# Three visits of the attention made whole, and a fourth half product that accumulates in an old bank

## Chip, cores and metric

The kernel runs on one core of one Trainium2 chip. The metric is device microseconds of that core; three runs of the kernel before gave 557.68, 557.76 and 559.34 us, the median is 557.76.

## What is computed

A causal attention with decay, in 4 batches, 8 heads, 768 tokens of 64, is followed by a feed-forward layer on the 3072 rows of 512 that it gives:

```
state = lam**64 * state + (k * decay).T @ v        # per head, block after block of 64 tokens
out   = tril(q @ k.T * decay) @ v + (q * decay) @ state
h     = max(out_rows @ w_in, 0)                    # 3072 x 512 @ 512 x 2048
y     = (h * h) @ w_out                            # 3072 x 2048 @ 2048 x 512
```

Products of the feed-forward layer are made of two halves of each operand (high and low part), three products each, to keep fp32 precision.

## The kernel before, in words

The tokens are cut into 24 chunks of 128. Eight chunks go through the feed-forward layer plainly, in three tiles (`ffn`, matmuls at L763 to L772). The other 16 form two **twins** of eight chunks. For a twin, four pairs of chunks stand side by side as 512 columns, and each of the two big products is done as a two-by-two block product with seven half products in place of eight. The sums of token rows that this needs are written by `pairs` into `pa`, `pz`, `ps`, `pt` (L847, L848, L855); the sums of weights are made by `differences` (L822 to L834), stored in HBM (`kept`, L812), and streamed back in pieces of 256 KB, one for each half product, into six buffers `b` (`streamed`, L870). SP issues these loads in the order of the products, and each waits for the product that last used its buffer.

`first_products` makes the hidden blocks of one pair j of weight blocks from the products 1 to 7. One **product** is six matmuls of 128x512 at L489. Products 1, 6 and 7 accumulate one after the other in the same PSUM bank, x, and ScalarE copies the bank's state away after each (`copy`, L891: r1, r2, r3). Product 2 has bank y, product 5 bank v; product 3 goes on top of 5 in v. A hidden block is the sum of a bank and a copy, made by VectorE (`block`, L895), and then ReLU and square on ScalarE (L896, L897). Product 4 has a bank of its own, z, and its block is z plus r3. `second_products` does the same for the second layer (splits at L942 and L943, sums at L950, ends at L1024).

The rest of the attention is done in between, in **visits**. A visit finishes two old chunks and opens two new ones: first half of the old results, opening of the first new chunk, second half of the old results, opening of the second new chunk, all of them small 64x64 matmuls at L489. Between the halves of the old results two tiny ScalarE copies out of the banks (L709, `dots`) order the second half behind the first. An opening is followed by VectorE work on its banks (L566, L575), a ScalarE copy of one bank (L559), and the finished results are scaled by L599. The loads of the next visit's chunks (L515, four of 512 KB: `ka` and `qv` of each chunk) wait for the buffers that this visit frees; `qv` is weighted by L539 when it lands.

Visits 1 to 8 are **parted**: the first half of the old results and the first opening are one stretch, the rest a second stretch, with four other pieces of TensorE's work between. Visits 6, 7 and 8 lie among the first twin's first products, before the products with the numbers in `INSIDE`, and their second stretch comes `LATER_BY` = 4 products later.

The order of instructions is static: `Plan.order` simulates the engines with costs written in the kernel and emits the program in the order that it finds. TensorE's order in the twins is fixed by `link`/`linked`; the order on the other engines follows from the plan's times and keys.

Of the kernel before, what the change touches and what calls it, by code (L numbers as in the profile page):

```python
# [13 lines left out]
AF = mybir.ActivationFunctionType  # L14
# [10 lines left out]
NF = DFF // P  # L25
# [11 lines left out]
WIDE, NARROW = 4 * C, 3 * C  # L37
# [192 lines left out]


VISITS = [(1, 8, 0), (1, 12, 1), (1, 14, 0)]
PARTED = {1: 1, 2: 1, 3: 1, 4: 1, 5: 1, 6: 1, 7: 1, 8: 1}
BETWEEN = {3: 3, 4: 7, 5: 11}
APART, LATER_BY = 3, 4
PAIR_LATER = [717, 726, 735, 753]
PAIR_AT = [7, 10, 13, 12]
INSIDE = {6: 9, 7: 31, 8: 52, 9: 63}

FIRST_ORDER = [1, 2, 6, 5, 7, 4, 3]  # L240
PARTS = 9
# [1 line left out]
N_RS = 2  # L243
DIFF_AT = [[440, 450, 530, 560, 565.5, 569.5, 573.5, 577.5], [590, 626, 630, 638, 646, 654, 662, 670]]
SPARE_FROM, SPARE_KEY = 16, 0.0
AT_ONCE = [1, 2, 4, 6, 5, 7, 3]
LAST_ORDER = [4, 1, 2, 6, 5, 7, 3]
KEPT = {1: 0, 2: 1, 5: 2, 4: 3, 7: 4, 6: 5, 3: 6}
A_PROD, PASS = 1.36, 10.9
# [23 lines left out]
def tt(n):  # L273

    return 0.066 + n / 960


def act(n):

    return 0.085 + n / 1200  # L280
# [13 lines left out]
def kernel(ctx: ExitStack, tc: tile.TileContext, ka, qv, lamx, w, out):  # L294
    nc = tc.nc
    ps = ctx.enter_context(tc.tile_pool(name="ps", bufs=1, space=PSUM))
    plan = Plan()
# [5 lines left out]
    def place(name, at, shape, dtype=F32):  # L303

        n = 1
        for m in shape:
            n *= m
        a = nc.alloc_sbuf_tensor_at(name, [P, n], dtype, offset=BASE + 4 * at).ap()
        if len(shape) == 2:
            a = a.rearrange("p (a b) -> p a b", a=shape[0])  # L310
        if len(shape) == 3:
            a = a.rearrange("p (a b c) -> p a b c", a=shape[0], b=shape[1])
        return a
# [61 lines left out]
    sums = {g: place(f"p{g}", REGIONS[f"p{g}"][0], [2, n, WIDE], F32R) for g, n in (("a", 4), ("z", 2), ("s", 4), ("t", 4))}  # L375
# [11 lines left out]
    def at(b):  # L387
        return tiles[b.kind][b.slot]
# [99 lines left out]
    def mm(*args, **kw):  # L488
        nc.tensor.matmul(*args, **kw, skip_group_check=True)  # L489
# [376 lines left out]
    def streamed(i, j, k, key):  # L866

        n_streams[i] += 1
        b = Buf("b2" if i == 0 and B2_FROM <= n_streams[0] <= 7 * B2_STEPS and n_streams[0] % 4 == 0 else "b")
        return b, in_turn("streamed", plan.op("SP", LOAD, key - 12, lambda: nc.sync.dma_start(out=at(b).bitcast(F32), in_=kept[i][j][KEPT[k]]), stored[i, j], [b], lat=3.2))  # L870

    def first_products(p, j, key):

        banks, r, h, made = {k: Buf("bank") for k in "xyvz"}, [Buf("u") for _ in range(3)], hidden[p], ready_h[p]
        where = {1: "x", 2: "y", 6: "x", 5: "v", 7: "x", 4: "z", 3: "v"}
        source = {1: ("a", 0), 2: ("a", 2), 4: ("z", 0), 6: ("s", 0), 3: ("s", 2), 7: ("t", 0), 5: ("t", 2)}
        st = {}

        def product(i, deps=()):
            (b, o), bank, (g, k) = streamed(0, j, i, key), banks[where[i]], source[i]  # L880

            def fn():
                x, first = sums[g][:, :, k:k + 2], i in (1, 2, 5, 4)
                for t, (u, v) in enumerate(((0, 0), (0, 1), (1, 0))):
                    for kb in range(2):
                        mm(at(bank), at(b)[:, u, kb * P:kb * P + P], x[:, v, kb], start=first and not t and not kb, stop=t == 2 and kb == 1)

            return link(plan.op("PE", A_PROD, key, fn, [o] + ready2[p][g] + list(deps), [b, bank, p_[p][g]], mode="F", entries=12))

        def copy(k, dst, o):  # L890
            return plan.op("ACT", act(WIDE) + 0.09, key - 6, lambda: nc.scalar.copy(at(dst), at(banks[k])), [o], [banks[k], dst])  # L891

        def block(k, t, f, a, deps):
            b = h[t, f]
            o = plan.op("DVE", tt(WIDE) + 0.1, key - 6, lambda: nc.vector.tensor_tensor(out=at(b), in0=at(banks[k]), in1=at(a), op=ALU.add), deps, [banks[k], b, a])  # L895
            o1 = plan.op("ACT", act(WIDE) + 0.12, key, lambda: nc.scalar.activation(at(b), at(b), AF.Relu), [o], [b])  # L896
            o1 = plan.op("ACT", act(WIDE) + 0.12, key, lambda: nc.scalar.activation(at(b), at(b), AF.Square), [o1], [b])  # L897
            made[t, f] = [o1]
            return o

        def run(i):
            f0, f1 = 2 * j, 2 * j + 1
            if i == 1:
                st["r1"] = copy("x", r[0], product(1))
            if i == 2:
                block("y", 0, f0, r[0], [product(2), st["r1"]])
            if i == 6:
                st["r2"] = copy("x", r[1], product(6, [st["r1"]]))
            if i == 5:
                st["p5"] = product(5)  # L910
            if i == 7:
                st["r3"] = copy("x", r[2], product(7, [st["r2"]]))
                st["v"] = block("v", 1, f1, r[2], [st["p5"], st["r3"]])
            if i == 4:
                st["p4"] = product(4)
            if "r3" in st and "p4" in st:
                block("z", 1, f0, r[2], [st.pop("p4"), st["r3"]])
            if i == 3:
                block("v", 0, f1, r[1], [product(3, [st["v"]]), st["r2"]])

        return run
# [119 lines left out]
    for f in range(NF):  # L1041
        t = FIRST + f * SLOW_STEP
# [5 lines left out]
    def place_of(v):  # L1048
        if v < len(VISITS):
            k, f, _ = VISITS[v]  # L1050
            return begin[k] + per[k] * f
        if v in BETWEEN:
            return begin[2] + per[2] * BETWEEN[v]
        return twice[0][0] + INSIDE[v] * A_PROD

    chunks = []
    for i in range(len(CHUNKS)):
        ti = PLACE[i][0]
        if i < N_ALONE:
            key = 0 if ti == 0 else BEGIN2  # L1060
        else:
            key = place_of((i - N_ALONE) // 2)
# [10 lines left out]
    def visiting(v, narrow, key, ahead=0):  # L1073
        old = later[max(0, 2 * v - 2):2 * v]
        chain = visit(old, later[2 * v:2 * v + 2], key, ahead, PARTED.get(v), narrow)
        for ch in old:
# [19 lines left out]
    for v, ((ti, f, ahead), chain) in enumerate(zip(VISITS, visits)):  # L1096
        chain[0].after += [steps[ti, f - ahead][2], steps[ti, f + 1][0]]
        steps[ti, f][1].after.append(steps[ti, f + 1][0])
        k = PARTED.get(v, -1)
        steps[ti, f + 1 - ahead][1].after.append(chain[k])  # L1100
        later_ = [steps[ti, f + 2][0]] if f + 2 < NF else [steps[ti + 1, g][0] for g in range(2)]
        if v in PARTED:
            chain[k + 1].after.append(steps[ti, f + 1 - ahead][1] if len(later_) == 1 else later_[0])
# [10 lines left out]
    def link(o):  # L1114
        o.after.append(end[0])
        end[0] = o
        return o

    def linked(chain):
        chain[0].after.append(end[0])  # L1120
        end[0] = chain[-1]
# [7 lines left out]
    while left:  # L1129
        g, k = left.pop(0)  # L1130
        link(steps[2, g][k])
        if k == 2 and g in visit_of:
            v = visit_of[g]
            chain = visiting(v, False, begin[2] + per[2] * g)
            n = PARTED.get(v)
            if n is None:
# [7 lines left out]
    hidden = [{(t, f): Buf(f"h{t}{f}") for t in range(2) for f in range(NF)} for _ in range(TWINS)]  # L1144
    ready_h, gate = [{} for _ in range(TWINS)], [[] for _ in range(TWINS)]
    visit_at = {k: v for v, k in INSIDE.items()}
    for p in range(TWINS):
        a, b = twice[p]
        runs = [first_products(p, j, a + 7 * A_PROD * j) for j in range(NF // 2)]
        order = [(j, i) for j in range(NF // 2) for i in (FIRST_ORDER if j or p else AT_ONCE)]  # L1150
        for j in range(1, NF // 2):
            k = order.index((j, 1))
            order[k - 1], order[k] = order[k], order[k - 1]
        n, rest = 0, []

        def visited():
            if rest and n == rest[0][0]:
                linked(rest.pop(0)[1])
            if p == 0 and n in visit_at:
                v = visit_at[n]  # L1160
                chain = visiting(v, False, a + A_PROD * n)
                k = PARTED.get(v, len(chain) - 1) + 1
                linked(chain[:k])
                if k < len(chain):
                    rest.append((n + LATER_BY, chain[k:]))

        product, after = second_products(p, b)
        for j, i in order:
            visited()
            if (j, i) == order[-1]:  # L1170
                product(LAST_ORDER[0], 0, b)
            runs[j](i)
            if j == NF // 2 - 1 and i in (2, 6, 3):
                gate[p].append(end[0])
            n += 1
            if p == 0 and n == 1:
                for k in tail:
                    link(steps[2, k[0]][k[1]])
        for k, i in enumerate(LAST_ORDER):
            for j in range(NF // 2):  # L1180
                visited()
                if k or j:
                    product(i, j, b + PASS * k + A_PROD * j)
                n += 1
            after(i)
# [63 lines left out]
```

## Time and profile before

| what | value |
|---|---|
| median of three runs | 557.76 us (557.68 to 559.34) |
| span of the profiled execution | 556.8 us |
| median less that span | 0.96 us |
| TensorE (PE) busy | 550.3 us |
| VectorE (DVE) busy | 440.8 us |
| ScalarE (ACT) busy | 339.1 us |
| mean granted TensorE clock | 0.999 |
| first twin's first products, with visits 6 to 8 | about 230 to 324 us of the span |

The profile page gives the span of the one execution that was profiled and no other time of it; the difference to the median is what lies around the span. The page's busy share of TensorE counts matmuls that overlap, so it tells only whether the engine stood empty. To see lost time, one takes the starts of matmuls: within a product they are 0.227 us apart, and a product starts 1.36 us after the one before it, unless something lies between.

### The profile page before, as it was taken

Reading aid. Unit: us, or ns where it says so; the run is one execution under the profiler, and the core shown is the slowest. Engines: PE = TensorE matmul, PEld = TensorE weight load, DVE = VectorE, ACT = ScalarE, POOL = GpSimd, SP = SyncE. Lnnn points to the kernel's source line nnn. Section 1 sums busy time; section 2 is a strip of 40 time slices with the busy share of each in tenths; the row PEclk is TensorE's granted clock in tenths of the full one; section 3 lists DMA queues with packets and bytes.
Section 4 is the critical chain, followed back from the end, with each engine's and each line's share of the span. In section 5 each row is a group of like instructions: output and inputs, shape, how many; then the busy total and the mean of one; then the engine's idle time right before and its main releaser. Section 6 shows DMA issues by size and latency. Waiting matters only on the chain.

```text
span 556.8 us, 12879 instructions
## 1 busy us (share of the span) xinstructions
PE 550.3 (99%) x4907; PEld 468.8 (84%) x4907; DVE 440.8 (79%) x867; ACT 339.1 (61%) x695; POOL 5.1 (1%) x10
## 2 busy tenths in 40 slices
PE   8999999999999999999999999999999999999997
PEld 7789899998989888888887888888888888888885
DVE  5998999997989899889686899998723235889664
ACT  5866677673644556576766856564366667754551
POOL 3000000000000000000000000000000000000000
PEclk9999999999999999999999999999999999999999
DMA  8999789875968577699989655776876666666765
GB/s 316 368 295 354 253 262 298 293 230 159 333 229 301 186 263 279 214 298 360 306 288 361 213 161 156 211 218 197 277 223 193 193 195 196 192 191 201 223 197 172
DMA packets 70141, 137.17 MB, mean 246 GB/s; under 512 B 7232, under 2 KB 19776, under 8 KB 70080
## 3 DMA queue, kind: packets, MB, share of 16 engines
q1 hardware_dynamic: 69792, 136.21, 75.6%
q8 instruction: 39, 0.64, 0.5%
q10 hardware_dynamic: 288, 0.14, 0.1%
q14 instruction: 22, 0.18, 0.1%
HBM read 100.67 MB, written 35.65 MB: 245 GB/s over the span
## 4 chain that ended last, share of the span: by engine, by line
PE 96%; DMA 2%; DVE 1%; SPq 0%; issue 0%; ACT 0%; DVEq 0%
PE bank L489 63%; PE bank L763 16%; PE bank L769 5%; PE bank L772 5%; PE bank L770 5%; DMA b<-kept 1%; DMA ka<-ka 1%; PE bank L747 1%; PE bank L742 1%; SPq L515 0%; DVE end L1024 0%; PE bank L408 0%; PE bank L425 0%; DVE h L895 0%; DVE pt L848 0%
## 5 line engine op out<-in xcount | busy, mean ns | idle before, releaser
L489 PE MATMUL bank<-v,b 128*128 128x512 f32 x672 | 153.4, 389 | 0.0
L489 PEld LDWEIGHTS bank<-v,b 128*128 128x128 f32 x672 | 126.0, 188 | 26.2
L942 ACT CAST v<-h 128x512 fp32r<-128x512 f32 x112 | 68.4, 621 | 56.9 <-PE bank L489 41.7
L895 DVE TENSOR_TENSOR h<-bank,u 128x512 f32<-128x512 f32 x64 | 44.1, 691 | 61.5 <-ACT u L891 33.3
L943 DVE TENSOR_TENSOR v<-h,v 128x512 fp32r<-128x512 f32 x112 | 75.9, 689 | 18.6 <-ACT v L942 9.2
L896 ACT ACTIVATE h<-h 128x512 f32<-128x512 f32 x64 | 40.2, 631 | 21.9 <-DVE h L895 19.5
L769 PE MATMUL bank<-wo,gh 128*128 128x512 f32 x125 | 49.3, 394 | 0.0
L489 PE MATMUL bank<-ps,b 128*128 128x512 f32 x192 | 49.1, 391 | 0.0
L489 PE MATMUL bank<-pa,b 128*128 128x512 f32 x192 | 48.8, 390 | 0.2 <-DMA b<-kept 0.2
L770 PE MATMUL bank<-wo,gh 128*128 128x512 f32 x125 | 49.0, 392 | 0.0
L891 ACT COPY u<-bank 128x512 f32<-128x512 f32 x48 | 28.0, 583 | 31.0 <-PE bank L489 30.8
L489 PE MATMUL bank<-pt,b 128*128 128x512 f32 x192 | 46.4, 390 | 0.0
L950 DVE TENSOR_TENSOR h<-h,h 128x512 f32<-128x512 f32 x64 | 43.0, 684 | 0.1
L489 PEld LDWEIGHTS bank<-pa,b 128*128 128x128 f32 x192 | 35.9, 188 | 8.0 <-DVE h L895 0.6
L489 PEld LDWEIGHTS bank<-ps,b 128*128 128x128 f32 x192 | 35.8, 188 | 7.9 <-DVE h L895 0.5
L489 PEld LDWEIGHTS bank<-pt,b 128*128 128x128 f32 x192 | 35.9, 188 | 7.5
L897 ACT ACTIVATE h<-h 128x512 f32<-128x512 f32 x64 | 38.5, 625 | 0.3
L763 PE MATMUL bank<-xb,wi 128*128 128x384 f32 x192 | 35.4, 336 | 0.0
L763 PEld LDWEIGHTS bank<-xb,wi 128*128 128x128 f32 x192 | 33.6, 188 | 0.9
L763 PE MATMUL bank<-xa,wi 128*128 128x384 f32 x180 | 34.0, 338 | 0.0
L763 PEld LDWEIGHTS bank<-xa,wi 128*128 128x128 f32 x180 | 31.6, 188 | 1.3 <-DVE work L463 0.2
L489 PE MATMUL bank<-qv,ka 64*64 64x64 f32 (+2 forms) x1040 | 26.8, 225 | 0.7 <-DMA ka<-ka 0.5
(152 smaller groups left out, 866.8 us busy)
## 6 DMA issues: line engine op xcount, KB each, us to landing
b<-kept SPq DMA_DIRECT2D x224, 256.0 KB, 2.9
work<-w SPq DMA_DIRECT2D x32, 512.0 KB, 4.8
ka<-ka SPq DMA_DIRECT2D x23, 512.0 KB, 5.4
qv<-qv SPq DMA_DIRECT2D x19, 512.0 KB, 5.5
kept<-part SPq DMA_DIRECT2D x36, 256.0 KB, 3.6
kept<-v SPq DMA_DIRECT2D x28, 256.0 KB, 4.4
kept<-wi SPq DMA_DIRECT2D x24, 256.0 KB, 3.9
kept<-wo SPq DMA_DIRECT2D x24, 256.0 KB, 3.7
```

The lines of the kernel that those rows point to most:

```text
L489: nc.tensor.matmul(*args, **kw, skip_group_check=True)
L763: nc.tensor.matmul(at(h)[:, 0:n], wt[:, cc, :], xt[:, cc, :], start=k == 0, stop=k == 3 * NCC - 1)
L769: nc.tensor.matmul(at(os_[j]), at(gh)[:, sl], woh[f], start=f == 0 and ti >= SINGLE, stop=False)
L770: nc.tensor.matmul(at(os_[j]), at(gh)[:, sl], wol[f], start=False, stop=False)
L772: nc.tensor.matmul(at(os_[j]), at(gl)[:, sl], woh[f], start=False, stop=f == NF - 1)
L891: return plan.op("ACT", act(WIDE) + 0.09, key - 6, lambda: nc.scalar.copy(at(dst), at(banks[k])), [o], [banks[k], dst])
L895: o = plan.op("DVE", tt(WIDE) + 0.1, key - 6, lambda: nc.vector.tensor_tensor(out=at(b), in0=at(banks[k]), in1=at(a), op=ALU.add), deps, [ ...
L896: o1 = plan.op("ACT", act(WIDE) + 0.12, key, lambda: nc.scalar.activation(at(b), at(b), AF.Relu), [o], [b])
L897: o1 = plan.op("ACT", act(WIDE) + 0.12, key, lambda: nc.scalar.activation(at(b), at(b), AF.Square), [o1], [b])
L942: oh = plan.op("ACT", act(WIDE) + 0.12, key - 16, lambda: nc.scalar.copy(rounded[hi.slot], at(b)), made[t, 2 * j + e], [b, hi], after)
L943: ol = plan.op("DVE", tt(WIDE) + 0.1, key - 16, lambda: nc.vector.tensor_tensor(out=rounded[lo.slot], in0=at(b), in1=rounded[hi.slot], op= ...
L950: made[o] = [plan.op("DVE", tt(WIDE) + 0.1, when, lambda: nc.vector.tensor_tensor(out=at(h[o]), in0=at(h[a]), in1=at(h[b]), op=op), deps + ...
```

## The change

Four edits. (1) Visits 6, 7 and 8 are no longer in `PARTED`: all four of their parts run in one stretch, before products 7, 29 and 49 in place of 9, 31 and 52 (and 4 later). (2) Product 4 loses its bank z and accumulates in bank x on top of 1, 6 and 7; it has to wait for the copy r3, and its block needs no sum on VectorE: ScalarE takes the ReLU straight from the bank. (3) The next pair's product 1 moves ahead by one more place, to between 7 and 4; the very first pair takes the usual order 1, 2, 6, 5, 7, 4, 3 in place of 1, 2, 4, 6, 5, 7, 3. (4) In the last pair the first of the second products stands ahead of 4 in place of ahead of 3, and the marks in the order (`gate`) that let the first splits start shift with it.

```diff
-PARTED = {1: 1, 2: 1, 3: 1, 4: 1, 5: 1, 6: 1, 7: 1, 8: 1}
+PARTED = {1: 1, 2: 1, 3: 1, 4: 1, 5: 1}
-INSIDE = {6: 9, 7: 31, 8: 52, 9: 63}
+INSIDE = {6: 7, 7: 29, 8: 49, 9: 63}
-AT_ONCE = [1, 2, 4, 6, 5, 7, 3]
+AT_ONCE = [1, 2, 6, 5, 7, 4, 3]
...
-        where = {1: "x", 2: "y", 6: "x", 5: "v", 7: "x", 4: "z", 3: "v"}
+        where = {1: "x", 2: "y", 6: "x", 5: "v", 7: "x", 4: "x", 3: "v"}
...
-                x, first = sums[g][:, :, k:k + 2], i in (1, 2, 5, 4)
+                x, first = sums[g][:, :, k:k + 2], i in (1, 2, 5)
...
-            o1 = plan.op("ACT", act(WIDE) + 0.12, key, lambda: nc.scalar.activation(at(b), at(b), AF.Relu), [o], [b])
-            o1 = plan.op("ACT", act(WIDE) + 0.12, key, lambda: nc.scalar.activation(at(b), at(b), AF.Square), [o1], [b])
-            made[t, f] = [o1]
+            squared(t, f, plan.op("ACT", act(WIDE) + 0.12, key, lambda: nc.scalar.activation(at(b), at(b), AF.Relu), [o], [b]))
             return o
+
+        def squared(t, f, o):
+            b = h[t, f]
+            made[t, f] = [plan.op("ACT", act(WIDE) + 0.12, key, lambda: nc.scalar.activation(at(b), at(b), AF.Square), [o], [b])]
...
             if i == 4:
-                st["p4"] = product(4)
-            if "r3" in st and "p4" in st:
-                block("z", 1, f0, r[2], [st.pop("p4"), st["r3"]])
+                b, o = h[1, f0], product(4, [st["r3"]])
+                squared(1, f0, plan.op("ACT", act(WIDE) + 0.12, key - 6, lambda: nc.scalar.activation(at(b), at(banks["x"]), AF.Relu), [o], [banks["x"], b]))
...
             k = order.index((j, 1))
-            order[k - 1], order[k] = order[k], order[k - 1]
+            order.insert(k - 2, order.pop(k))
...
-            if (j, i) == order[-1]:
+            if (j, i) == order[-2]:
                 product(LAST_ORDER[0], 0, b)
             runs[j](i)
-            if j == NF // 2 - 1 and i in (2, 6, 3):
+            if j == NF // 2 - 1 and i in (2, 7, 4):
                 gate[p].append(end[0])
```

**First place: TensorE at the start of the first twin, up to visit 6.** A row with `pa`, `pz`, `ps` or `pt` is a product (the sum of tokens that it reads, and its streamed buffer `b`); 64x64 rows belong to the visit. Before:

```order
L489 MATMUL bank_62<-pa,b_167 128x512 x6
L489 MATMUL bank_63<-pz,b_168 128x512 x6
L489 MATMUL bank_60<-ps,b_169 128x512 x6
L489 MATMUL bank_64<-pt,b_170 128x512 x6
L489 MATMUL bank_60<-pt,b_171 128x512 x6
L489 MATMUL bank_58<-pa,b_166 128x512 x6
L489 MATMUL bank_64<-ps,b_0_172 128x512 x6
L489 MATMUL bank_61<-pa,b_167 128x512 x6
L489 MATMUL bank_65<-work,qv_111 64x64 x2
```

These are products 2, 4, 6, 5, 7, the next pair's 1, then 3, the next pair's 2, and the first row of the visit. With the change:

```order
L489 MATMUL bank_62<-pa,b_167 128x512 x6
L489 MATMUL bank_60<-ps,b_168 128x512 x6
L489 MATMUL bank_63<-pt,b_169 128x512 x6
L489 MATMUL bank_60<-pt,b_170 128x512 x6
L489 MATMUL bank_64<-pa,b_171 128x512 x6
L489 MATMUL bank_60<-pz,b_166 128x512 x6
L489 MATMUL bank_58<-work,qv_111 64x64 x2
```

Now the products are 2, 6, 5, 7, the next pair's 1, and 4 in the bank of 6 and 7; then the visit starts, and product 3 comes behind the whole of it. Inside that visit the first opening (`qv_110,ka_108`) is now followed at once by the second half of the old results:

```order
L489 MATMUL bank_65<-qv_110,ka_108 64x64 x2
L489 MATMUL bank_59<-qv_110,ka_108 64x64 x2
L489 MATMUL bank_65<-qv_110,ka_108 64x64 x8
L489 MATMUL bank_58<-work,qv_111 64x64 x2
L489 MATMUL bank_61<-work 64x64 x2
```

Four products stood at this joint before.

**Second place: ScalarE around the same visit.** `small` rows are the two copies that the second half of the old results waits for. Before:

```order
L896 ACTIVATE h_0_200<-h_0_200 128x512
L897 ACTIVATE h_0_201<-h_0_201 128x512
L897 ACTIVATE h_0_200<-h_0_200 128x512
L896 ACTIVATE h_0_185<-h_0_185 128x512
L897 ACTIVATE h_0_185<-h_0_185 128x512
L709 COPY small<-bank_65 128x1
L709 COPY small<-bank_59 128x1
```

With the change:

```order
L891 COPY u_221<-bank_64 128x512
L896 ACTIVATE h_0_201<-h_0_201 128x512
L833 CAST v_230<-ob_106 128x256
L918 ACTIVATE h_0_200<-bank_60 128x512
L901 ACTIVATE h_0_201<-h_0_201 128x512
L709 COPY small<-bank_58 128x1
L709 COPY small<-bank_61 128x1
```

L918 is the ReLU of product 4's block straight from the bank, and L901 the square; the two copies stand directly behind them.

**Third place: SP's queue behind visit 7,** where the loads for visit 8 (`ka`, `qv`) stand among the streamed loads `b` and the stores of weight sums (`kept`). Before:

```order
L515 DMA ka_108<-ka 128x1024
L870 DMA b_167<-kept_159 128x512
L812 DMA kept_160<-v_230 128x512
L812 DMA kept_160<-v_231 128x512
L870 DMA b_168<-kept_159 128x512
L812 DMA kept_160<-v_229 128x512
L870 DMA b_169<-kept_159 128x512
L870 DMA b_170<-kept_159 128x512
L515 DMA qv_110<-qv 128x1024
L515 DMA ka_109<-ka 128x1024
L515 DMA qv_112<-qv 128x1024
L870 DMA b_171<-kept_159 128x512
```

With the change:

```order
L870 DMA b_170<-kept_159 128x512
L812 DMA kept_160<-v_226 128x512
L515 DMA ka_108<-ka 128x1024
L515 DMA qv_110<-qv 128x1024
L515 DMA ka_109<-ka 128x1024
L870 DMA b_171<-kept_159 128x512
L515 DMA qv_112<-qv 128x1024
L870 DMA b_166<-kept_159 128x512
```

The four loads now stand together, with one streamed load ahead of the last; before, one stood apart and three together.

## Rows read from the trace of the kernel before

**Rows 1.** The page's head and part 1: busy time of each engine.

```profile
span 556.8 us, 12879 instructions
...
PE 550.3 (99%) x4907; PEld 468.8 (84%) x4907; DVE 440.8 (79%) x867; ACT 339.1 (61%) x695; POOL 5.1 (1%) x10
```

**Rows 2.** Chain of waits, 226 to 400 us: start us, length us, what.

```profile
232.82 6.81 PE bank L489 x30
...
239.66 0.60 ACT u L891
...
240.28 0.70 DVE h L895
...
241.02 48.76 PE bank L489 x670
...
289.80 6.81 DMA b<-kept
...
296.75 103.40 PE bank L489 x789
```

**Rows 3.** Timeline of PE around visit 6's first stretch: start us, length us.

```profile
239.46 1.52 PE L489 MATMUL bank<-pa,b 128*128 128x512 f32 x6
241.02 1.66 PE L489 MATMUL bank<-ps,b 128*128 128x512 f32 x6
242.52 1.52 PE L489 MATMUL bank<-pa,b 128*128 128x512 f32 x6
243.97 0.27 PE L489 MATMUL bank<-work,qv 64*64 64x64 f32 x2
...
244.07 0.23 PE L489 MATMUL bank<-work,qv 64*64 64x64 f32 x2
...
244.13 0.23 PE L489 MATMUL bank<-work,qv 64*64 64x64 f32 x2
...
244.95 1.11 PE L489 MATMUL bank<-qv,ka 64*64 64x64 f32 x48
245.99 1.66 PE L489 MATMUL bank<-ps,b 128*128 128x512 f32 x6
247.49 2.88 PE L489 MATMUL bank<-pt,b 128*128 128x512 f32 x12
```

**Rows 4.** Timeline of PE at the end of visit 6's second stretch.

```profile
252.64 1.11 PE L489 MATMUL bank<-qv,ka 64*64 64x64 f32 x64
253.69 1.66 PE L489 MATMUL bank<-pa,b 128*128 128x512 f32 x6
```

**Rows 5.** Timeline of PE, 294 to 301 us.

```profile
295.05 1.52 PE L489 MATMUL bank<-pz,b 128*128 128x512 f32 x6
296.75 1.62 PE L489 MATMUL bank<-pa,b 128*128 128x512 f32 x6 [0.18 <-DMA b<-kept]
298.21 1.54 PE L489 MATMUL bank<-ps,b 128*128 128x512 f32 x6
299.59 1.52 PE L489 MATMUL bank<-pa,b 128*128 128x512 f32 x6
```

**Rows 6.** Groups of ACT, 230 to 320 us (busy us, mean ns | idle before), and one timeline row.

```profile
L896 ACT ACTIVATE h<-h 128x512 f32<-128x512 f32 x31 | 19.3, 630 | 9.5 <-DVE h L895 8.9
L833 ACT CAST v<-ob 128x256 fp32r<-128x256 f32 x28 | 10.5, 404 | 1.6 <-DVE ob L830 1.5
L709 ACT COPY small<-bank 128x1 f32<-128x1 f32 x6 | 0.7, 161 | 0.3 <-PE bank L489 0.3
...
241.50 1.16 ACT L896 ACTIVATE h<-h 128x512 f32<-128x512 f32 x2
```

**Rows 7.** Landing of the L515 loads, and stretches: PE busy, clock, DMA share, GB/s.

```profile
DMA to landing us min/median/max: 3.6/5.5/8.4
...
24.00:32.00 8.00, 8.00 (x161) 1.00 0.85 290
...
251.60:253.80 2.20, 2.20 (x130) 1.00 1.03 370
```

More of the change, by code (lines that the diff above doesn't have):

```diff
@@ L872, in first_products @@
     def first_products(p, j, key):
-        banks, r, h, made = {k: Buf("bank") for k in "xyvz"}, [Buf("u") for _ in range(3)], hidden[p], ready_h[p]
-        where = {1: "x", 2: "y", 6: "x", 5: "v", 7: "x", 4: "z", 3: "v"}
+        banks, r, h, made = {k: Buf("bank") for k in "xyv"}, [Buf("u") for _ in range(3)], hidden[p], ready_h[p]
+        where = {1: "x", 2: "y", 6: "x", 5: "v", 7: "x", 4: "x", 3: "v"}
         source = {1: ("a", 0), 2: ("a", 2), 4: ("z", 0), 6: ("s", 0), 3: ("s", 2), 7: ("t", 0), 5: ("t", 2)}
```

## The prediction, on record before the result was known

> **What bounds the kernel now.** I read the page first: TensorE is busy 550.3 of 556.8 us, VectorE 440.8, ScalarE 339.1 [rows 1]. So work taken from VectorE is worth nothing by itself; only what lets TensorE start its matmuls earlier counts. Busy time can't show that, as matmuls overlap, so I went on to the chain of waits in the stretch that the change touches. There the chain is TensorE alone but for two places: at 239.66 it leaves TensorE for a copy r3 on ScalarE and a block sum on VectorE, and at 289.80 for a streamed load of 6.81 us [rows 2]. Last I read TensorE's timeline and measured from start to start. A product takes 1.36 us (six times 0.227; 30 matmuls in 6.81 us [rows 2]). From 296.75 on, the first twin's 103.4 us of chain have no wait but the borders of visits [rows 2]. So the change can save only what these starts show as lost.
>
> **Borders of a stretch.** At visit 6's first stretch four things are lost [rows 3, 4]. The product ahead of it takes 242.52 to 243.97, 1.45 us, 0.09 too much. Its small matmuls come in fours, 0.06 us apart (244.07 to 244.13), but the first four take 0.10: 0.04 lost. At the end of the second stretch 64 matmuls from 252.64, sixteen fours of 0.058, would be issued by 253.58; the next product starts at 253.69: 0.11 lost. That product, as 245.99 to 247.49 shows, takes 1.50 us: 0.14 lost. Together 0.38 us for each stretch, whatever its length. Three visits become one stretch each in place of two: 3 x 0.38 = **1.14 us** saved. The small matmuls stay the same, 2.02 us a stretch (243.97 to 245.99), so a whole visit takes about 4.0.
>
> The new joint, first opening then second half of the old results, is in no row. The nearest joint is that from the half results to the opening inside a stretch: 244.95 follows in the same rhythm, at no cost [rows 3]. The other end is a border, 0.38. I take nothing, since both sides of the joint are 64x64 matmuls as in the nearest row. The Trainium skill says the same in "TensorEngine Tiling (Array Packing)", Key Properties: changing the tiling mode drains the engine, changing only the tile doesn't; by it, too, the joint is free.
>
> **First wait, 240.8 us.** Product 3 of the first pair should have started at 239.46 + 1.36 = 240.82 and started at 241.02: 0.20 lost, and it took 1.50, 0.14 more [rows 3]. It waited for the block sum in bank v, which waited for r3 (0.60, then 0.70 [rows 2]); the order gave it one product (the next pair's 1) as cover, 1.36 us, too little for 0.16 of matmul tail, 0.60, 0.70 and three handovers of some 0.03. In the new order the next pair's 1 and product 4, then all of visit 6, stand between 7 and 3: the wait goes, **0.34 us** saved.
>
> **Second wait, 296.4 us.** The product after 295.05 was due at 296.41, started at 296.75 and took 1.46, the next one 1.38 [rows 5]: 0.34 + 0.10 + 0.02 = **0.46 us** lost to a streamed load issued behind visit 8's big loads [rows 2]. A buffer b is refilled when its product ends and used again five products later, so a load has 6.8 us, less about 0.2; 6.81 is just too long. With the change three of four big loads can be issued inside visit 7, when TensorE uses no b. Walk it from the visit's start, T: `ka` at T + 2.0 (after the first opening), `qv` at T + 3, `ka` at T + 4, b_171 when the first product behind the visit ends, T + 5.6, the other `qv` behind it, b_166 at T + 7. The shortest landing of such a load is 3.6 us, and at the 370 GB/s of a full stretch 512 KB take 1.4 us and 256 KB 0.7 [rows 7]. With 0.7 for a store ahead of it `ka` lands by T + 6.3, then 7.7, 9.1, b_171 at 9.8, `qv` 11.2, b_166 11.9. Needed: b_171 at T + 4.2 + 6 x 1.36 = T + 12.4, b_166 at T + 13.7. Some 2 us are left, which cover two or three more stores. I take the wait as gone. The bounds are all of it kept, and a stall longer by one more 512 KB in the bunch, 1.4.
>
> **Product 4 in bank x.** It removes 16 sums on VectorE of 0.70 [rows 2], 11.2 us, worth nothing on the path (VectorE is not what TensorE waits for once the first wait is gone). It adds a wait of TensorE for r3, 16 times, with one product between 7 and 4. The copy starts at once in the trace (product 7's last matmul, then 239.66 [rows 2]): 0.16 of tail, 0.60 of copy, two handovers, 0.84 in all against 1.36. Each has 0.5 us to spare, so nothing; the cover is that next product 1 (the first second product in the last pair). The same distance stands between 6 and 7 in the kernel before, 16 times, and the chain shows no wait there. What is late next if the copy is late is product 4 and all of TensorE behind it.
>
> **The whole visit.** Its second half needs the two tiny copies. For visit 6: product 4 now stands at 239.46, the visit starts at 240.91, and the first opening ends at 242.93. ScalarE has, from 239.62 on, a copy (0.60), a ReLU (0.63), a cast (0.40, which waits for VectorE), the ReLU from the bank, not before 240.98, a square, and two copies of 0.16 [rows 6]. One behind the other the last ends at 242.8; as two ReLUs take 1.16 [rows 6], not 1.26, it is earlier. Margin 0.1 to 0.4 us, so nothing, but thin; the bound is one ScalarE operation late. The banks hold: six for the visit, one for v, one for the next x, and the second opening's last bank is x, free after that ReLU, 2 us ahead. All four loads must be in at the start of a visit; they have 22 products, some 30 us. The second products' first splits have three products of cover in place of four, 4.1 us against two operations of about 0.7: nothing.
>
> **Sum.** 1.14 + 0.34 + 0.46 = 1.94 us, all in the span: 556.8 to 554.9. The median stands 0.96 above the span, so 557.76 - 1.94 = **555.8 us**, 0.35% faster. About 0.3%, 1.7 us, is what a measurement of this kernel can tell from no change, so this lies on its edge.
>
> **Rivals.**
> - *The tiny copies come late.* One ScalarE operation (0.63) less the margin, some 0.4, plus 0.14 for the restart, 0.54 a visit: 1.6 given back, 557.4. For it: the square stands ahead of them in the queue, and a cast that waits for VectorE. Against: the margin. In part, 0.4 to 1.6, chance 0.19.
> - *The streamed loads still wait.* 0.46 stays: 556.3; with the longer bunch 557.2. For it: four loads together, where three were too many. Against: the walk. Chance 0.15.
> - *The joint costs a border,* 3 x 0.38: 557.0. Chance 0.04.
> - *Slower: product 4 waits for r3.* The order on ScalarE is new, and the first twin's casts [rows 6] can stand ahead of a copy. Two operations ahead of it (0.63 + 0.40) make 0.84 into 1.87, 0.51 over the cover, with 0.14 of restart 0.65 for each product 4. In all eight pairs of the first twin that is 5.2 us: 561.0. It decides against the change once the 16 average over 0.23 us, as 1.94 + 1.7 are then used up. Chance 0.08.
> - *Slower: the clock falls.* A stretch of small matmuls twice as long could let the granted clock drop to 1.2 GHz. Against: it was 1.00, the 2.4 GHz level, through 251.6 to 253.8 and through 24 to 32 us, eight microseconds of small matmuls [rows 7]. At half rate for three products behind each visit it would cost 3 x 4.1 = 12.2 us: 568.0. Chance 0.02. The rule behind it is in the Trainium skill, "TensorE: Matmul & The Clock Gate", Part 1: the half rate is the default and activity releases it; the rows here speak against a fall.
>
> That the change doesn't do what it says is out: the order shows it.
>
> **How the numbers follow.** The forecast has 0.52: all three gains, 555.3 to 556.3 with the run's own scatter, of which 0.46 lie beyond 0.3% (below 556.1). The tiny copies, the loads and the joint (0.38) end within 0.3%, as does the upper end of the forecast (0.06). The two slower cases hold 0.10. The range goes from 555.3 to 557.4, the whole price of the late copies, and leaves out about 0.12.
>
> **What would show it.** Right: in TensorE's timeline one stretch of about 4.0 us for each of visits 6 to 8, with its parts unbroken; no gap near 241 and none from a load near 290 to 300; VectorE's L895 down from 64 to 48 with no change elsewhere; second twin unchanged. Wrong: waits of TensorE for L709, for L891 ahead of `pz` products, or for `b<-kept`, or a granted clock below 1.00 behind a visit.

## The result: slower, 564.33 us

Six runs of the changed kernel took 562.38 to 566.21 us, median 564.33; six of the kernel before, 557.68 to 559.34, median 557.82. The ratio is 1.0112, with the interval 1.0098 to 1.0126: the change costs 6.5 us (564.33 less 557.82), where the forecast was a gain of 1.94. The profiled run took 564.42 us with a span of 562.3, 5.5 longer than before [rows 1]. Between a run's time and its span lie 1.7 to 2.2 us in all profiled runs of this study; the 0.96 in the prediction came from the median and another execution's span, and nothing hangs on it, as the sum was a difference. That difference is 2.1 in all six runs of the changed kernel and 1.7 to 1.8 in the runs of the kernel before, so some 0.4 of the 6.5 us lies outside the span, where no run shows a cause.

The page of the changed kernel: head, busy time, the queue that carries instructions, the chain's shares, and the group of the block sums.

```profile
span 562.3 us, 12859 instructions
...
PE 551.5 (98%) x4907; PEld 470.7 (84%) x4907; DVE 430.6 (77%) x851; ACT 338.3 (60%) x695; POOL 5.1 (1%) x10
...
q8 instruction: 39, 0.64, 0.4%
...
PE 98%; issue 1%; DVE 0%; DVEq 0%
...
L895 DVE TENSOR_TENSOR h<-bank,u 128x512 f32<-128x512 f32 x48 | 33.2, 691 | 69.4 <-ACT u L891 33.9
```

VectorE lost its 16 sums and some 10 us, as intended, and TensorE's busy time is 1.2 us up [rows 1]. In the chain "issue" has grown from 0 to 1%: time in which TensorE waited for nothing that the profile shows. TensorE's list of waits in the changed kernel (who waited for whom: us in total, times, longest us) has four of these, 5.4 us together, and one wait of the program's start:

```profile
PE bank L489 <- issue: 5.4, 4, 2.5
PE bank L408 <- DVE ob L392: 1.5, 1, 1.5
```

The chain of waits in the stretch of [rows 2] says where:

```profile
232.76 10.88 PE bank L489 x189
243.65 2.48 issue
246.13 35.66 PE bank L489 x375
281.79 1.19 issue
282.98 31.70 PE bank L489 x378
314.68 1.56 issue
316.24 103.90 PE bank L489 x643
```

The detours over ScalarE, VectorE and the streamed load [rows 2] are gone; in their place stand three **stops** of TensorE, 2.48, 1.19 and 1.56 us, 5.23 in all, one in each whole visit. TensorE's timeline in visit 6 (start us, length us) answers to [rows 3, 4]:

```profile
241.83 0.94 PE L489 MATMUL bank<-qv,ka 64*64 64x64 f32 x42
...
243.37 0.28 PE L489 MATMUL bank<-qv,work 64*64 64x64 f32 x2
246.13 0.27 PE L489 MATMUL bank<-work 64*64 64x64 f32 x2 [2.48 <-issue]
...
246.52 1.82 PE L489 MATMUL bank<-qv,ka 64*64 64x64 f32 x62
248.28 2.46 PE L489 MATMUL bank<-ps,b 128*128 128x512 f32 x6
```

And in visit 7:

```profile
280.21 1.11 PE L489 MATMUL bank<-qv,ka 64*64 64x64 f32 x64
281.15 0.65 PE L489 MATMUL bank<-s,qv 64*64 64x64 f32 x32
282.98 0.34 PE L489 MATMUL bank<-qv,hold 64*64 64x64 f32 x8 [1.19 <-issue]
```

The joint itself is free: 281.15 follows the opening in the same rhythm. The stop comes deeper, in the middle of the second half of the old results; in visit 6 matmuls on both sides of it read tiles of the same names. And behind visit 6's stop things are slow: 62 small matmuls take 1.82 us where 64 took 1.11 [rows 4], the product 2.46 where it took 1.66 [rows 3]. The stretches of the changed kernel show why (busy time of PE, PEld, DVE, ACT, POOL, then granted clock, DMA share, GB/s):

```profile
241.00:243.60 2.60, 2.60 (x156) 2.51 (x152) 1.04 (x3) 2.58 (x8) 0.00 (x0) 1.00 0.97 314
243.60:246.10 2.50, 0.05 (x1) 0.00 (x0) 0.47 (x2) 0.00 (x0) 0.00 (x0) 1.00 0.96 318
246.10:250.00 3.90, 3.87 (x88) 3.46 (x89) 2.71 (x6) 0.00 (x0) 0.00 (x0) 0.57 0.62 210
```

The granted clock was 1.00, the 2.4 GHz level, up to and through the stop, and fell to the 1.2 GHz level behind it. Before the change it was 1.00 through the second stretch of the same visit [rows 7]. The fall cost some 0.7 us on the small matmuls and 0.8 on the product, 1.5. Where a run's mean clock stayed 1.000 the time was 562.38 us, still 4.6 over the kernel before; at 0.995 and 0.996 it was 564.0 to 564.7, at 0.993 566.21.

The sum of the trace: from the first small matmul to the product behind it, the visits take 7.43, 5.31 and 5.78 us, 18.52, where a parted one took 2 x 2.02 [rows 3], 12.12 for three: 6.4 more, the slow small matmuls included. Add 0.8 for the slow product. Off go 0.6 for the borders of stretches (0.2 us in the wide matmuls between two stretches, three fewer) and 0.8 for the two old waits (0.34 and 0.46). That makes +5.8; the span grew by 5.5.

### The profile page after: what moved, and what is told of

Its sections match the earlier page's. It is cut to its first block, busy times and chain, and to the rows that moved or that the text cites. A ratio compares the mean times of both kernels' runs of the same rounds, so it can differ in the third digit from the quotient of the medians.

```text
span 562.3 us, 12859 instructions
## 1 busy us (share of the span) xinstructions
PE 551.5 (98%) x4907; PEld 470.7 (84%) x4907; DVE 430.6 (77%) x851; ACT 338.3 (60%) x695; POOL 5.1 (1%) x10
## 4 chain that ended last, share of the span: by engine, by line
PE 98%; issue 1%; DVE 0%; DVEq 0%
PE bank L489 64%; PE bank L763 16%; PE bank L769 5%; PE bank L770 5%; PE bank L772 5%; PE bank L408 1%; PE bank L747 1%; PE bank L742 1%; DVE end L1025 0%; PE bank L425 0%; DVE ob L392 0%; DVEq L1237 0%
## 5 line engine op out<-in xcount | busy, mean ns | idle before, releaser
L895 DVE TENSOR_TENSOR h<-bank,u 128x512 f32<-128x512 f32 x48 | 33.2, 691 | 69.4 <-ACT u L891 33.9
L896 ACT ACTIVATE h<-h 128x512 f32<-128x512 f32 x48 | 30.4, 633 | 25.1 <-DVE h L895 24.1
L901 ACT ACTIVATE h<-h 128x512 f32<-128x512 f32 x64 | 38.9, 628 | 0.3
```

The source lines that it names most:

```text
L896: squared(t, f, plan.op("ACT", act(WIDE) + 0.12, key, lambda: nc.scalar.activation(at(b), at(b), AF.Relu), [o], [b]))
L901: made[t, f] = [plan.op("ACT", act(WIDE) + 0.12, key, lambda: nc.scalar.activation(at(b), at(b), AF.Square), [o], [b])]
```

## What the stops are: instructions that come late

**Theory** ("code theory" in the expectations). TensorE's instructions come in pieces of 256, and at a stop the next piece has not come yet. The three stops stand before the instructions 5825, 6593 and 7361 of TensorE, counted from 0 in the trace (weight loads, matmuls, waits). They are 768 = 3 x 256 apart. The place between two pieces is called a border of 256 below, or border alone; it is another thing than the border of a stretch. The page has 39 transfers of instructions with 0.64 MB, 16 KB each, for some 10,000 instructions of TensorE: one for every 256. A parted stretch issues 224 or 256 instructions (112 or 128 matmuls with their weight loads) in 2.02 us and then has four products of 1.36 us; a whole visit issues 480 or 512 within 4, so it needs two pieces of code 2 us apart. In the kernel before, borders of 256 came 2.9 us apart or more, everywhere.

**Rivals.** A hidden wait of the visit's second half (for a copy, a bank, a load) that the trace has not named ("hidden-wait theory"): then the stop is bound to a matmul, not to a number. And product 4 that waits for the copy r3, as in the prediction ("product-4 theory").

### Moving the numbers

32 one-column matmuls are added early in TensorE's program:

```diff
     def turned():
+        for _ in range(32):
+            nc.tensor.matmul(at(rps)[0:P, 0:1], zero[:, 0:P], zero[:, 0:1], start=True, stop=True)
```

> The changed kernel with 32 one-column matmuls (64 instructions of TensorE with their weight loads) added in the first 15 us; they write columns of a bank that the next matmuls overwrite. Code theory: the stops in visits 6 to 8 stand 32 matmuls earlier in each visit, again before an instruction whose number in TensorE's stream is 193 above a multiple of 256. Hidden-wait theory: the stops stay before the same matmuls of the visits. The start may take 1 to 2 us longer.

One run took 575.46 us, of which 11 us are a longer start (with the clock at 0.5 for 10 us there). The added matmuls count four instructions each in the trace, so the numbers moved by 128. The chain (lines of the kernel are two further):

```profile
255.86 2.45 issue
...
294.03 1.53 issue
...
327.14 1.02 issue
```

The stops did not stay at their matmuls. They moved 63 or 64 matmuls on, to the instructions 6081, 6849 and 7617, the old numbers plus 256, out of the second half of the old results into the second opening. The hidden wait falls. My expectation had the distance wrong, the grid not.

### Less traffic beside the code

Half of the streamed bytes of most loads between the 12th and the 56th are left out (the products then read old values in the other half):

```diff
+        part = i == 0 and 12 <= n_streams[0] <= 56 and (n_streams[0] % 4 or n_streams[0] > 28)
...
-... nc.sync.dma_start(out=at(b).bitcast(F32), in_=kept[i][j][KEPT[k]]) ...
+... nc.sync.dma_start(out=at(b)[:, 0:1].bitcast(F32) if part else at(b).bitcast(F32), in_=kept[i][j][KEPT[k]][:, 0:1] if part else kept[i][j][KEPT[k]]) ...
```

> The changed kernel with streamed loads of half the bytes (the high parts alone; the low parts of the weights stay those of an earlier product) from the 12th to the 56th, but for some early ones: half of the streamed bytes among visits 6 to 8 are left out. Code theory, with pieces that queue behind data: the piece for visit 6 comes sooner than 4.6 us, its stop falls from 2.5 us to 1 to 1.5, the others by less; 562 or below. If the wait for a piece is a fixed latency: stops as in the changed kernel, 564.

561.87 us, ratio 1.0065 (1.0044 to 1.0087), mean clock 1.000. The chain:

```profile
243.74 1.74 issue
...
279.62 1.23 issue
...
312.53 1.17 issue
```

The stops are 0.74 us shorter, 0.04 longer and 0.39 shorter. The time fell below 562 as the theory had it; the first stop stayed over the 1 to 1.5 us forecast. So traffic can make a piece later, but most of the wait is there with half of the streamed bytes too.

### How late a piece is

Over the changed kernel and all kernels of the study, 19 stops in the visits or right behind them are over 0.25 us. All of them stand before an instruction whose number, counted from 0, is 193 above a multiple of 256, and none of these 19 instructions has a wait for a semaphore. Each stop ended 1.22 to 1.59 us after the 16 KB packet (the transfer that brings a piece) had come in. Nine of them (from the trace's records; us):

```
                       packet         TensorE    after the
kernel, visit          begins  ends   goes on    packet    stop
changed, 6             243.72 244.67  246.13     1.46      2.48
changed, 7             280.34 281.61  282.98     1.37      1.19
changed, 8             313.89 315.02  316.24     1.22      1.56
numbers moved, 6       256.04 256.93  258.31     1.38      2.45
half the load, 6       243.18 244.06  245.48     1.42      1.74
whole alone, 7         279.71 280.58  282.17     1.59      2.00
one product apart, 6   242.90 244.85  246.20     1.35      1.37
6 and 8 whole, 8       311.45 312.45  313.81     1.36      0.60
whole, later, 7        289.75 290.67  292.10     1.43      1.90
```

In the changed kernel the packet began 2.4, 0.6 and 1.4 us after the border before, and took 0.95 to 1.27. With some 1.4 behind it, a piece took 4.82, 3.23 and 3.71 us from border to border. Four whole visits of the runs below had no stop over 0.25 us: there the packet began 0.1 to 1.5 us before TensorE reached the first border, early enough for the second.

### The parts of the change apart

All visits parted again, the rest as changed:

```diff
-PARTED = {1: 1, 2: 1, 3: 1, 4: 1, 5: 1}
+PARTED = {1: 1, 2: 1, 3: 1, 4: 1, 5: 1, 6: 1, 7: 1, 8: 1}
```

> The change with visits 6 to 8 parted again (four products between), all else as changed. If TensorE's instructions arrive too late in whole visits (code theory): no stop inside a visit, the two old waits gone, 557.8 - 0.34 - 0.46 = 557.0. If product 4 in bank x waits for the copy r3 (product-4 theory): it stays slow, 561 to 564. If the visits wait for a semaphore that whole visits only bring forward (hidden-wait theory): 557.0 as well.

559.47 us, ratio 1.0021 (1.0012 to 1.0029); the ratios are to runs of the kernel before in the same series, with medians of 557.9 to 558.5. No stop, no fall of the clock: of the 1.12% that the change costs, 0.91 go with the whole visits. The two old waits are gone too, but a new one takes their place. The end of its chain before the long rest:

```profile
293.27 3.83 DMA kept<-v
...
297.18 0.59 ACT u L891
...
297.81 122.28 PE bank L489 x873
```

Product 4 waits for the copy r3, and the copy waits for a store: its buffer is one of eight (`u` in the kernel) that the weight sums use too, and the store of such a sum had not ended. It is the rival "product 4 waits for r3", by another way than ScalarE's queue, and at one place for 0.9 us in place of 16. In the changed kernel it waits nowhere. The 557.0 was missed: 0.8 less than the kernel before in this series (558.4) is 557.6. Of the 1.9 us over that, 0.9 are this wait and 0.35 lie outside the span (2.1 against 1.76 us); some 0.6 stay open.

With `LATER_BY` 1 or 2 in place of 4 besides, one or two products stand between the stretches:

> The change with visits 6 to 8 parted by one product in place of none. Code theory: 256 instructions of a stretch then take 2.0 + 1.4 + 0.4 = 3.8 us; the stops of 2.9 us and 3.3 us from one piece of code to the next vanish, the one of 4.6 us leaves 0.8: 557.0 to 558, no fall of the clock. Hidden-wait theory: what is left of the wait stands at the first matmul of the second stretch.

> The change with visits 6 to 8 parted by two products. Code theory: 5.2 us from piece to piece, over the 4.6 seen: no stop, 557.0, the same as with four products. Hidden-wait theory: the same time. Product-4 theory: 561 to 564.

One product: 559.48 us, ratio 1.0019 (1.0008 to 1.0030). Two: 559.25, ratio 1.0008 (0.9995 to 1.0021). Both times miss the forecast, as with four products; the stops bear on the theory. The chain with one product has the stop of visit 6, 1.11 us shorter, and 0.09 us in visit 8:

```profile
244.83 1.37 issue
246.20 66.53 PE bank L489 x754
312.72 0.09 issue
```

That is close to what the theory asks: a product of 1.36 us takes about that much off each stop, 2.48 to 1.37 (1.12 worked out from the 2.48; the expectation had 0.8), 1.19 and 1.56 to 0 and 0.09 (0 and 0.2). With two products the stops are down to 0.12 us at most; there a streamed load came late, and TensorE stood for 1.97 us between two products with the granted clock at 1.00 before and behind:

```profile
PE bank L489 <- DMA b<-kept: 2.0, 1, 2.0
```

The other part alone, whole visits at their old places with product 4 in its own bank:

```diff
-PARTED = {1: 1, 2: 1, 3: 1, 4: 1, 5: 1, 6: 1, 7: 1, 8: 1}
+PARTED = {1: 1, 2: 1, 3: 1, 4: 1, 5: 1}
```

> The kernel before with visits 6 to 8 whole, nothing else changed. Code theory: three stops of 1 to 2.5 us inside the visits, 5 us in all, perhaps a fall of the clock, less 1.14 for the borders: 561 to 565. Product-4 theory: 557.8 - 1.1 = 556.7. Hidden-wait theory: stops too, but at the first matmul behind the joint.

559.54 us, ratio 1.0021 (1.0007 to 1.0035). Without product 4's edit it is slower all the same, against the product-4 theory. But the code theory's 561 to 565 us was missed too; the chain has one stop, not three:

```profile
240.47 39.69 PE bank L489 x527
280.17 2.00 issue
282.17 137.87 PE bank L489 x1027
```

Behind it the clock fell (columns as for the changed kernel's stretches):

```profile
282.20:286.00 3.80, 3.80 (x109) 3.55 (x109) 2.63 (x7) 0.00 (x0) 0.00 (x0) 0.55 0.57 184
```

### Does the place decide?

Only visit 7 stopped there. So visit 7 parted and 6 and 8 whole at the old places; without and with product 4's edit; and that edit with all visits parted at the old places:

> The kernel before with visits 6 and 8 whole and visit 7 parted, all at their old places. Code theory (a whole visit stops only where its second border of 256 instructions comes less than about 2.9 us behind the first one and the piece's packet began late): with all three whole at these places only visit 7 stopped, so here no stop over 0.5 us in any visit, no stretch at granted clock 0.5, and 557.0 to 557.8 us (before, less up to two borders of 0.38 us), ratio 0.998 to 1.000. If every whole visit stops wherever it stands, or stops come and go with the runs: 1.2 to 2.5 us in visit 6 or 8, 559 to 561 us.

> The changed kernel with visit 7 parted again and the three visits back at their old places (9, 31, 52), product 4 in the bank of 1, 6 and 7 as changed. Code theory: no stop in the visits, no clock fall; if product 4's copy wait (1.04 us in the first experiment) belonged to the earlier places it is gone and the time is 556.3 to 557.2 us, ratio 0.997 to 0.999; if it stays, 557.2 to 558.2. If stops come in any whole visit: 559 to 562 us.

> The changed kernel with all visits parted and back at their old places: product 4's edit with its order alone. No stop in the visits under any theory. If the edit gains its two old waits (0.34 and 0.46 us) and product 4 waits for nothing: 557.0 us, ratio 0.9985. If product 4 waits for the copy r3 as in the first experiment (about 1 us, once): 557.8 to 558.5 us, ratio 1.000 to 1.002.

| kernel | median us | ratio to before | stops in visits 6, 8 |
|---|---|---|---|
| 6 and 8 whole | 558.06 | 0.9994 (0.9982 to 1.0005) | none, 0.60 |
| the same with product 4's edit | 557.97 | 0.9992 (0.9983 to 1.0002) | 0.49, none |
| product 4's edit, all parted | 558.64 | 0.9998 (0.9988 to 1.0009) | none |

No clock fell, but stops of half a microsecond come and go between visits at the same place. The first kernel's ratio is within its forecast, its stop 0.1 us over the 0.5 allowed; the second has a stop where none was forecast, and the waits of the last two are not the copy's that their forecasts named. In the last two kernels TensorE waits near 297 us, where the streamed load was late before [rows 5]; the lists of waits:

```profile
PE bank L489 <- DMA b<-kept: 1.0, 1, 1.0
PE bank L489 <- issue: 0.5, 1, 0.5
```

```profile
PE bank L489 <- ACT h L896: 1.3, 1, 1.3
```

In the last one it is the load as well: TensorE's own wait for the load's semaphore ends at 297.28, behind a landing at 297.25, while the ReLU named ends at 297.30 and is nothing that product 4 needs. The second old wait was not removed by the new order there. It is absent where visit 7 stops, and in two kernels where it doesn't (one product apart; 6 and 8 whole in the old order), so what removes it is not shown.

Then all three visits whole at later places, for the kernel before (with `PARTED` as in the change) and the changed one, whose edit is shown:

```diff
-INSIDE = {6: 7, 7: 29, 8: 49, 9: 63}
+INSIDE = {6: 13, 7: 37, 8: 57, 9: 63}
```

> The kernel before with visits 6 to 8 whole, put 4, 6 and 5 products later (13, 37, 57), so that the first border of 256 instructions comes 8, 8 and 16 matmuls behind a visit's start, not 44 to 64 as in the changed kernel. Code theory with position: the piece for the second border is asked for sooner against the visit, its packet begins 0.3 to 1 us sooner, so stops of 0 to 0.8 us a visit, no granted clock of 0.5, and 556.8 to 558.2 us. If only the 480 to 512 instructions in 4 us count, wherever the borders lie: 1.2 to 2.5 us in each visit as in the changed kernel, 560 to 563 us.

> The changed kernel with its three whole visits at 13, 37 and 57 in place of 7, 29 and 49, product 4 as changed. Code theory with position: stops of 0 to 0.8 us a visit, no granted clock of 0.5; with the gains of the prediction (1.14 and up to 0.80 us) less the stops and, if product 4's wait for the copy stays, about 1.2 us: 556.0 to 557.8 us. If the place of the borders does not count: 561 to 564.5 us.

561.48 us, ratio 1.0047 (1.0031 to 1.0064), and 562.87, ratio 1.0076 (1.0063 to 1.0089). Two of three visits now run through in 3.89 us, but the time is lost all the same. The chain of the first of these kernels:

```profile
254.65 0.51 issue
...
290.20 1.90 issue
...
326.35 0.52 issue
```

My expectation failed. Counted with all instructions, the first border lies 2 to 4 us ahead of these visits, the next one 112 to 120 matmuls into them, and the third at 241 to 248. So it falls at the last 15 matmuls of visit 7, 1.90 and 2.19 us in the two kernels, and right behind visits 6 and 8, where wide products follow, 0.3 to 0.9 us. Its place moves the stop and changes its size; with 480 or more instructions in 4 us it did not go away here. Why a packet begins sooner or later against its border is not settled.

No kernel of the study beats the one before by more than 0.1%, within what can be told apart.

## Why the prediction was wrong, point by point

- **Failed: the whole visit.** "The small matmuls stay the same ... so a whole visit takes about 4.0": the three took 7.43, 5.31 and 5.78 us. The joint, for which "I take nothing", costs nothing; what was not priced is the supply of instructions. The rows for it [rows 3, 4] were stretches of at most 256 instructions with products behind them, so none of them could show two pieces 2 us apart. The page before had the count of transfers, 39, in the line below, and the planner's own constant `FETCH` = 4.5 us per 256 instructions, used for the first 40 us only, names a price. Measured: 5.23 us of stops and 1.5 of clock.

```profile
q8 instruction: 39, 0.64, 0.5%
```

- The Trainium skill has the block in "Runtime: NRT & Kernel Launch", Instruction fetch mechanics: instruction memory is refilled in blocks of 16 KiB, 256 instructions, while the present ones run, and the crossing is mostly hidden. The 39 packets agree with the block. Most crossings cost nothing here, but those in the whole visits cost 1.19 to 2.48 us: in dense small matmuls "hidden" does not hold, and the measurement decides.
- **Borders of a stretch: right.** 3 x 0.38 was forecast. A whole visit without a stop took 3.89 us (visits 6 and 8 at the later places) against 4.04, and one border of 0.20 fewer: 0.35 a visit. In the changed kernel the stops hide it.
- **First wait [rows 3]: right.** No wait near 241 in the changed kernel.
- **Second wait: right for the changed kernel, for less reason than I gave.** It has no load wait, but its stop also gave the loads time. Of the six kernels without a stop in visit 7, three have a load wait of 1.0 to 2.0 us, one the copy's 0.9, two neither. The walk was too tight, and that the new order removes the wait is not shown.
- **Product 4 in bank x: right in the changed kernel**, wrong by 0.9 us at one place with the visits parted.
- **Tiny copies: in time.** In the changed kernel they end at 242.27, 0.29 us ahead of the second half of the old results in visit 6, within the forecast margin of 0.1 to 0.4. ScalarE's copies [rows 6] and TensorE's first row of that half:

```profile
242.05 0.22 ACT L709 COPY small<-bank 128x1 f32<-128x1 f32 x2
...
242.56 0.27 PE L489 MATMUL bank<-work,qv 64*64 64x64 f32 x1
```

- **Rivals.** None named the instructions. "The clock falls" had 0.02 and a price of 12.2 us; it fell once, for 1.5 us, and after a stop, not from the small matmuls. The sign rested on one cost that no rival held, and the chance of slower, 0.10, was too low.

## What to carry to other kernels

Before you join dense stretches of small matmuls, count TensorE's instructions, weight loads included, and mark each 256th. Where two borders come closer than a piece takes (3.2 to 4.8 us in the changed kernel, 2.7 to 5.4 over all 19 stops), price the wait for the next piece; it may be less or none, as in the four whole visits whose packet began early; the work between two stretches that looks like a mere interruption may be its cover. When the chain says "issue", compare the instructions' numbers before blaming a semaphore.

## What the runs showed of the hardware

A piece of code holds 256 instructions: 19 of 19 stops stood at a border of 256, and TensorE went on 1.2 to 1.6 us after the packet's end. The granted clock fell to 0.5 behind the five stops of 1.90 to 2.48 us, and behind none of the fourteen of 0.30 to 1.74; the wait of 1.97 us for a load between two products left it at 1.00. A one-column fp32 matmul counted as four instructions in the trace, the small 64x64 ones as two.
